# Attention with a three-way maxout layer on one core: another order of the work in batch 0

## The chip, the core and the metric

The kernel runs on one core of a Trainium2 chip. Five engines work side by side, each through its own instructions in order: TensorE (PE in the profile; its weight loads are PEld), VectorE (DVE), ScalarE (ACT), GpSimd (POOL) and SyncE (SP, which here only issues DMAs). They wait for each other by semaphores. The metric is the device time of one execution in microseconds, the median of the runs.

## The reference

q, k and v have 8 batches, 12 heads, 448 rows and a head dimension of 64, in float32. An attention whose denominator has one more term, exp(-m), is followed by a maxout layer of width 768:

```python
scores = scale * np.matmul(q, k.transpose(0, 1, 3, 2))
m = np.max(scores, axis=-1, keepdims=True)
e = np.exp(scores - m)
attn = e / (np.sum(e, axis=-1, keepdims=True) + np.exp(-m) + 1e-09)
attn_out = np.matmul(attn, v)          # (8, 12, 448, 64)
x = attn_out.transpose(0, 2, 1, 3).reshape(8 * 448, 12 * 64)
h = np.maximum(np.maximum(x @ w1, x @ w2), x @ w3)
out = h @ w_out                        # (3584, 768)
```

Multiplied by exp(m), the quotient is exp(scores) over (sum of exp(scores) + 1). The kernel computes it so, without a maximum, and the + 1 is the bias of a logarithm.

## The kernel before, in words

The 96 heads are worked in 48 pairs, six pairs to a batch. One round of the loop (`it`, L452) computes the scores of pair `it` and the attention products of the pair before it (`prev`). From it 6 on, products of the maxout layer of finished batches are put between the attention steps ("groups", L443), and PE is nearly always busy. In batch 0 (its 0 to 5) there is no such work yet. `keep_busy` (L345) puts products of a zero tile into PE there, 13 at the start, 3 after the first transposes, and 3 in each of its 0 to 4; their results are not used.

The 448 rows of a head are seven chunks of 64. Three full blocks of 128 rows, c = 0, 1, 2, and one last block of 64 rows are treated apart. A pair in batch 0 passes through these steps:

- `load` (L83): each of q, k and v comes with two DMAs, one for each half of the partitions. All are issued by SP, in program order, but for two at the very start that ACT issues. Pairs 1 and 2 share their v load, and pairs 4 and 5 share their loads. The raw tiles hold three pairs each and there are three of them, so pairs 0 to 2, 3 to 5 and 6 to 8 have a tile of their own.
- `casts` (L161): DVE turns q (L183), k (L184) and two small last blocks of k (L189) into 16 bits; POOL scales v (`scaled`, L157), with three operations.
- `transposes` (L204): PE transposes q and k block by block into PSUM (L221, L226), and DVE copies the result into qkT (L233). Pair 0's copy is split between DVE (L230) and ACT (L231).
- `scores` (L235) for each c: two products (L239), one a head, then `exp_scores` (L248) on ACT over both heads. `scores_last` (L251, product L255) and `exp_last` (L264) do the last block.
- `sums_main` and `sums_last` (L313, L324): six products and one closing product each, first for the denominators (`den`), then with v (`av`).
- `reciprocals_one` (L333): on ACT, the logarithm of (den + 1) into `lnd`, and exp of its negative into `rb`.
- `normalize_one` (L340): DVE multiplies av by rb into xT, the input of the maxout layer.

PSUM has two buffers for the scores (`ps_s`, used in turn by scores and scores_last), two that den and av share (`ps_av`, used in turn), and two for transposes, keep_busy and the maxout products (`ps_u`). qk16, the input of the transposes, has two buffers; vst, the scaled v, three.

An it of batch 0 before the change has this order in the program, and so on each engine: casts of the next pair; scores and exps of c = 0 and 1; den products of the pair before; score c = 2; av products; scores_last; both closing products; exp of c = 2; exp_last; logarithm and reciprocal; transposes of the next pair; keep_busy; normalize_one of the pair before. In it 5, three up products of the maxout layer follow the transposes, then the attention products of pair 5 itself.

The weights come on POOL's own DMA queue (`load_weight`, L144): the first in halves in its 3 and 4, the others in its 5, 6 and 8. POOL issues them in order with its scaling of v. In its 3 and 4, DVE clears a part of the raw q tile (L462) and SP then loads pairs 7 and 8 (and v of pair 6 in it 3).

Of the kernel before, what the change touches and what calls it, by code (L numbers as in the profile page):

```python
# [12 lines left out]
AF = mybir.ActivationFunctionType  # L13
# [8 lines left out]
def kernel(  # L22
# [11 lines left out]
    nc = tc.nc  # L34

    B, H, S, D = q.shape
# [6 lines left out]
    NPAIR = H // 2  # L43
# [39 lines left out]
    def load(p0, n_pairs, names="qkv", engs=(nc.sync, nc.sync)):  # L83
        b, j = divmod(p0, NPAIR)
        tiles = raw[(p0 // HB) % NRAW]
        h0 = 2 * (p0 % HB)
        for name, t, src in zip("qkv", tiles, (q, k, v)):
            if name not in names:
                continue
            rows = src[b, 2 * j : 2 * (j + n_pairs)].rearrange("h (p c) d -> p h c d", c=TP)  # L90
            hs = slice(h0, h0 + 2 * n_pairs)
            engs[0].dma_start(out=t[0:64, hs, 0 : NB + 1, :], in_=rows[:, :, 0 : NB + 1, :])
            engs[1].dma_start(out=t[64:128, hs, 0:NB, :], in_=rows[:, :, NB + 1 : TP, :])
# [7 lines left out]
    load(2, 1, "qk")  # L101
    load(1, 2, "v")
    load(3, 1, "qk")
    load(4, 2, "q")
    load(3, 1, "v")
    load(4, 2, "k")
    load(4, 2, "v")

    idle = cpool.tile([128, S], MMDT, name="idle")
# [51 lines left out]
    def casts(p):  # L161
        cast_qk(p)
        scale_v(p)
# [40 lines left out]
    def transposes(p):  # L204
        odd = (p // NPAIR) % 2
        qkT = att_pool.tile([2 * D, 1024], MMDT, tag="qkT", bufs=3)
        qkTs[p] = qkT, 0, S
        if p >= P_DMA:
            nc.sync.dma_start_transpose(
                out=qkT.rearrange("q (c p) -> q c p", p=128),  # L210
                in_=qk16[p % NK].rearrange("p c h d -> p (c h d)"),
            )
            qkTs[p] = qkT, 64 * odd, 512
            return
        trT = ps_u.tile([128, 1024], MMDT, tag="u", name="trT")


        order = (NB, 0, 1, 2) if odd else (0, 1, 2, NB)
        n0 = 0
        for c in order:  # L220
            nc.tensor.transpose(  # L221
                out=trT[:, n0 : n0 + 128], in_=q16[p % NK][:, c], identity=ident16
            )
            n0 += SL if c == NB else 128
        for c in range(NB + 1):
            nc.tensor.transpose(  # L226
                out=trT[:, S + c * 128 : S + c * 128 + 128], in_=k16[p % NK][:, c], identity=ident16
            )
        if p == 0:
            nc.vector.tensor_copy(out=qkT[:, 0 : S + 128], in_=trT[:, 0 : S + 128])  # L230
            nc.scalar.copy(out=qkT[:, S + 128 : S + 512], in_=trT[:, S + 128 : S + 512])  # L231
        else:
            nc.vector.tensor_copy(out=qkT[:, 0 : S + 512], in_=trT[:, 0 : S + 512])  # L233

    def scores(p, c):  # L235
        qkT, q0, k0 = qkTs[p]
# [11 lines left out]
    def exp_scores(p, c, stp):  # L248
        nc.scalar.activation(out=eT[:, p % 2, c], in_=stp[:, :, 0:S], func=AF.Exp, scale=scale)  # L249
# [80 lines left out]
            stop=True,  # L330
        )

    def reciprocals_one(den):  # L333
        lnd = small.tile([128, S], FP32, tag="lnd")
        rb = small.tile([128, S], FP32, tag="rb")
        nc.scalar.activation(out=lnd, in_=den[:, 0:S], func=AF.Ln, bias=1.0)
        nc.scalar.activation(out=rb, in_=lnd, func=AF.Exp, scale=-1.0)
        return rb

# [5 lines left out]
    def keep_busy(n):  # L345

        ps = ps_u.tile([128, 512], FP32, tag="u", name="busy")
        for _ in range(n):
            nc.tensor.matmul(out=ps[:, 0:S], lhsT=idle[:, 0:128], rhs=idle, start=True, stop=True)  # L349
# [95 lines left out]
            queue.pop(0)()  # L445

    LEFT = 4
    keep_busy(13)
    casts(0)
    transposes(0)  # L450
    keep_busy(3)
    for it in range(NP + 1):  # L452
        p = it if it < NP else None
        prev = it - 1 if it > 0 else None
        to_next = NPAIR - it % NPAIR
        n_groups = -(-max(len(queue) - LEFT, 0) // to_next) if it % NPAIR else 4
        n_groups = max(3, min(5, n_groups))

        first = {3: 1, 4: 2}.get(it)
        if first is not None:  # L460
            hs = slice(2 * first, 2 * first + 2)
            nc.vector.memset(raw[2][0][64:128, hs, NB - 1 : NB + 1, :], 0.0)  # L462
            if first == 1:
                load(NPAIR, 1, "v")
            load(NPAIR + first, 1)
        if it in (3, 4):
            load_weight(0, it - 3)
        if it in (5, 6, 8):
            load_weight((5, 6, 8).index(it) + 1)
        if it < NPAIR:  # L470

            casts(it + 1)
            for c in range(2):
                exp_scores(p, c, scores(p, c))
            if prev is None:
                keep_busy(3)
                exp_scores(p, 2, scores(p, 2))
                transposes(1)
                exp_last(p, scores_last(p))
            else:  # L480
                den, av = (ps_av.tile([128, 512], FP32, tag="av", name=n) for n in ("den", "av"))
                sums_main(prev, den, 1)
                stp = scores(p, 2)
                sums_main(prev, av, 0)
                stl = scores_last(p)
                sums_last(prev, den, 1)
                sums_last(prev, av, 0)
                exp_scores(p, 2, stp)
                exp_last(p, stl)
                rb = reciprocals_one(den)  # L490
                transposes(it + 1)
            if it < NPAIR - 1:
                keep_busy(3)
            else:

                ups = [up_open()]
                up_part(ups[0], 0, 0, 0, range(3))
                av5 = ps_s.tile([128, 2, 512], FP32, tag="s", name="av5")
                sums_main(p, av5[:, 1], 1)
                sums_main(p, av5[:, 0], 0)  # L500
                sums_last(p, av5[:, 1], 1)
                sums_last(p, av5[:, 0], 0)
                rb5 = reciprocals_one(av5[:, 1])
            if prev is not None:
                normalize_one(prev, av, rb)
            if it == NPAIR - 1:
                normalize_one(p, av5[:, 0], rb5)
                batch_done(0)
        elif it == NPAIR:
            exp_scores(p, 0, scores(p, 0))  # L510

            up_part(ups[0], 0, 0, 0, (3,))
            ups.append(up_open())
            up_part(ups[1], 0, 0, 1, range(4))
            ups.append(up_open(ps_av, "av"))
            up_part(ups[2], 0, 0, 2, range(4))
            for dc in (4, 5):
                for fc, ps in enumerate(ups):
                    up_part(ps, 0, 0, fc, (dc,))
                    if dc == 5:  # L520
                        up_close(ps, 0, 0, fc)
            del queue[0:3]
            exp_scores(p, 1, scores(p, 1))
            group()
            casts(it + 1)
            exp_scores(p, 2, scores(p, 2))
            exp_last(p, scores_last(p))
            group()
            transposes(it + 1)
            group()  # L530
        else:
            late = it + 1 < P_DMA
            if not late:

                if it + 2 < NP:
                    cast_qk(it + 2)
                    transposes(it + 2)
                if it + 1 < NP:
                    scale_v(it + 1)
            if p is not None:  # L540
                for c in range(2):
                    exp_scores(p, c, scores(p, c))
            group()
            if late:
                casts(it + 1)
            avs = [av_main(prev, hh) for hh in range(2)]
            av_last(prev, avs)
            if p is not None:
                stp = scores(p, 2)
                stl = scores_last(p)  # L550
            rb = reciprocals(prev, avs)
            if p is not None:
                exp_scores(p, 2, stp)
                exp_last(p, stl)
            if late:
                transposes(it + 1)
            group()
            normalize(prev, 0, avs, rb)
            group()
            normalize(prev, 1, avs, rb)  # L560
            if it % NPAIR == 0:
                batch_done(prev // NPAIR)
            if it + 2 == P_DMA:
                cast_qk(it + 2)
                transposes(it + 2)
            for _ in range(n_groups - 3):
                group()

        for n in range(NPAIR + HB, 2 * NPAIR) if it == NPAIR else (it + 5,):
            if it >= NPAIR and n < NP:  # L570
                load(n, 1)
# [32 lines left out]
```

## Time and profile before

| | |
|---|---|
| median of 3 runs | 367.61 us (367.52 to 367.77) |
| the profiled execution's own time | 367.07 us |
| its span, from first to last instruction | 365.3 us |
| granted TensorE clock, mean | 0.999 |
| PE busy in the span | 357.4 us |
| ACT busy in the span | 221.1 us |
| first exp of pairs 0 to 5 starts at | 7.64, 10.79, 15.09, 19.39, 23.69, 27.99 us |
| transposes of pair 6 start at | 30.52 us |
| first score of pair 6 starts at | 33.37 us |

Times inside the profile are counted from the start of the span. The profile's page gives busy times of engines and groups of instructions; the timeline lists instructions of one engine in order (start, length, engine, line, operation, shapes, count, and in brackets the idle time before and what ended it); the chain of waits follows back from the last instruction what released each step. A group of several pipelined instructions has one length, from the first one's start to the last one's end. Landing is when a DMA's data has arrived.

The loads of batch 0 as the DMA view has them (issue to landing): k of pair 2 landed at 10.91 us, k of pair 3 at 15.18, q of pairs 4 and 5 at 17.64, v of pair 3 at 18.52, k of pairs 4 and 5 at 21.18, their v at 22.81, k of pair 6 at 27.50. The halves of the first weight were issued by POOL at 19.67 and 23.98 and landed at 27.49 and 33.09; the second weight was issued at 25.96, landed at 40.82, and its first product ran at 42.50.

### The profile page before, as it was taken

Reading aid. Unit: us, or ns where it says so; the run is one execution under the profiler, and the core shown is the slowest. Engines: PE = TensorE matmul, PEld = TensorE weight load, DVE = VectorE, ACT = ScalarE, POOL = GpSimd, SP = SyncE. Lnnn points to the kernel's source line nnn. Section 1 sums busy time; section 2 is a strip of 40 time slices with the busy share of each in tenths; the row PEclk is TensorE's granted clock in tenths of the full one; section 3 lists DMA queues with packets and bytes.
Section 4 is the critical chain, followed back from the end, with each engine's and each line's share of the span. In section 5 each row is a group of like instructions: output and inputs, shape, how many; then the busy total and the mean of one; then the engine's idle time right before and its main releaser. Section 6 shows DMA issues by size and latency. Waiting matters only on the chain.

```text
span 365.3 us, 6122 instructions
## 1 busy us (share of the span) xinstructions
PE 357.4 (98%) x2086; PEld 163.9 (45%) x2086; DVE 243.4 (67%) x521; ACT 221.1 (61%) x335; POOL 53.6 (15%) x159
## 2 busy tenths in 40 slices
PE   8999999999999999999999999999999999999995
PEld 3434444444444444444444444444444444445552
DVE  4474777876578677577657867757666776555553
ACT  4996476765666766666567666666566766651000
POOL 4263112211211211211121121121112112000000
PEclk9999999999999999999999999999999999999999
DMA  5999997668667888849764896758675673005006
GB/s 151 229 234 229 233 247 211 155 177 214 161 180 182 208 184 154 195 107 185 182 173 122 178 200 164 175 133 214 159 174 137 165 208 83 5 2 131 2 0 172
DMA packets 87951, 58.61 MB, mean 160 GB/s; under 512 B 43504, under 2 KB 84464, under 8 KB 87920
## 3 DMA queue, kind: packets, MB, share of 16 engines
q1 hardware_dynamic: 83632, 53.18, 59.7%
q0 software_dynamic: 3920, 4.72, 7.5%
q10 hardware_dynamic: 368, 0.33, 0.4%
q8 instruction: 16, 0.26, 0.3%
q14 instruction: 15, 0.12, 0.1%
HBM read 42.47 MB, written 11.01 MB: 146 GB/s over the span
## 4 chain that ended last, share of the span: by engine, by line
PE 91%; ACT 2%; DMA 2%; DVE 2%; issue 1%; SPq 0%; DVEq 0%
PE up L356 44%; PE op L390 15%; PE av L273 13%; PE stp L239 8%; PE stl L255 4%; PE av L285 3%; DMA kin<-in_k_dram 2%; PE busy L349 2%; ACT eT L249 1%; PE trT L221 1%; PE trT L226 1%; PE av L316 1%; DVE qkT L233 1%; DVE o_sb L415 0%; DVE qk L183 0%
## 5 line engine op out<-in xcount | busy, mean ns | idle before, releaser
L356 PE MATMUL up<-xT,w 128*128 128x448 f16 x864 | 175.3, 353 | 0.7 <-DVE xT L307 0.4
L249 ACT ACTIVATE eT<-stp 128x896 f16<-128x896 f32 x144 | 125.5, 910 | 53.3 <-PE stp L239 53.3
L356 PEld LDWEIGHTS <-w 128*128 128x128 f16 x864 | 81.7, 98 | 81.7 <-issue 12.5
L372 DVE TENSOR_TENSOR hT<-hT,up 128x448 f16<-128x448 f16 x96 | 59.6, 621 | 52.1 <-PE up L356 51.1
L157 POOL TENSOR_SCALAR vst<-vin 128x384 f16<-128x384 f32 x132 | 43.1, 338 | 255.2 <-issue 159.2
L298 ACT ACTIVATE lnd<-av 64x448 f32<-64x448 f32 x84 | 45.3, 539 | 49.0 <-PE av L285 48.0
L390 PE MATMUL op<-w,hT 128*128 128x384 f16 x336 | 59.3, 326 | 0.0
L273 PE MATMUL av<-eT,vst 128*128 128x448 f16 x252 | 54.5, 352 | 0.0
L307 DVE TENSOR_TENSOR xT<-av,rb 64x448 f16<-64x448 f32 x84 | 51.8, 617 | 1.4
L239 PE MATMUL stp<-qkT 64*128 64x448 f16 x288 | 44.1, 353 | 1.5 <-DVE qkT L233 0.7
L370 DVE CAST hT<-up 128x448 f16<-128x448 f32 x48 | 29.8, 624 | 22.9 <-PE up L356 22.2
L415 DVE TENSOR_SCALAR o_sb<-op 128x384 f32<-128x384 f32 (+1 forms) x56 | 30.8, 550 | 20.0 <-PE op L390 19.0
L390 PEld LDWEIGHTS <-hT 128*128 128x128 f16 x336 | 31.6, 98 | 24.7 <-issue 4.0
L273 PEld LDWEIGHTS <-vst 128*128 128x128 f16 x252 | 24.7, 98 | 22.4
L184 DVE CAST qk<-kin 128x384 f16<-128x384 f32 x47 | 25.7, 548 | 1.1 <-DMA kin<-in_k_dram 0.7
L265 ACT ACTIVATE eL<-stl 128x448 f16<-128x448 f32 x48 | 25.9, 539 | 0.0
L299 ACT ACTIVATE rb<-lnd 128x448 f32<-128x448 f32 x42 | 24.2, 576 | 1.3
L239 PEld LDWEIGHTS <-qkT 64*128 64x128 f16 x288 | 11.0, 94 | 23.2 <-issue 16.5
L419 ACT ACTIVATE o_sb<-op 128x192 f32<-128x192 f32 x1 | 0.3, 331 | 30.2 <-DVE o_sb L415 30.2
L189 DVE CAST qk<-kin 64x64 f16<-64x64 f32 x94 | 17.5, 187 | 1.3
L255 PE MATMUL stl<-qkT 128*128 128x448 f16 x48 | 17.4, 362 | 0.0
L285 PE MATMUL av<-eL,vst 64*128 64x448 f16 x84 | 15.2, 359 | 0.0
(50 smaller groups left out, 117.7 us busy)
## 6 DMA issues: line engine op xcount, KB each, us to landing
out_dram<-o_sb SPq DMA_DIRECT2D x54, 192.0 KB, 2.8
qin<-in_q_dram SPq DMA_DIRECT2D x46, 128.0 KB, 3.0
kin<-in_k_dram SPq DMA_DIRECT2D x45, 128.0 KB, 2.9
vin<-in_v_dram SPq DMA_DIRECT2D x44, 128.0 KB, 2.9
kin<-in_k_dram SPq DMA_DIRECT2D x46, 96.0 KB, 2.7
qin<-in_q_dram SPq DMA_DIRECT2D x45, 96.0 KB, 2.7
vin<-in_v_dram SPq DMA_DIRECT2D x44, 96.0 KB, 2.8
w<-in_moe_w_dram POOLq DMA_DIRECT2D x2, 1152.0 KB, 17.1
```

The lines of the kernel that those rows point to most:

```text
L157: nc.gpsimd.tensor_scalar(out=out, in0=in_, scalar1=LAMBDA, scalar2=1.0, op0=ALU.mult, op1=ALU.mult)
L239: nc.tensor.matmul(out=stp[:, hh, 0:S], lhsT=qkT[hh * D : hh * D + D, k0 + c * 128 : k0 + c * 128 + 128], rhs=qkT[hh * D : hh * D + D, q0 ...
L249: nc.scalar.activation(out=eT[:, p % 2, c], in_=stp[:, :, 0:S], func=AF.Exp, scale=scale)
L255: nc.tensor.matmul(out=stl[:, 0, 0:S], lhsT=qkT[:, k0 + NB * 128 : k0 + NB * 128 + 128], rhs=qkT[:, q0 : q0 + S], start=True, stop=True,)
L273: nc.tensor.matmul(out=av[:, 0:S], lhsT=vst[:, p % VB, hh * NB + c, (1 - hh) * D : (3 - hh) * D], rhs=eT[:, p % 2, c, hh, :], start=(c == ...
L298: nc.scalar.activation(out=lnd[mine], in_=avs[hh][other, 0:S], func=AF.Ln, bias=1.0)
L307: nc.vector.tensor_tensor(out=xTs[b][mine, j, :], in0=avs[hh][mine, 0:S], in1=rb[mine], op=ALU.mult)
L356: nc.tensor.matmul(out=ps[:, 0:S], lhsT=w_sb[i][:, dc, ts(fc, 128)], rhs=xTs[b][:, dc, :], start=(dc == 0), stop=(dc == NDC - 1),)
L370: nc.vector.tensor_copy(out=h, in_=ps[:, 0:S])
L372: nc.vector.tensor_tensor(out=h, in0=h, in1=ps[:, 0:S], op=ALU.max)
L390: nc.tensor.matmul(out=ps[:, 0:NW], lhsT=hTs[sb][:, fc, ts(t, 128)], rhs=wout_sb[:, fc, ts(nh, NW)], start=(fc == 0), stop=(fc == NFC - 1),)
L415: nc.vector.tensor_scalar(out=o_sb[:, cs], in0=src, scalar1=1.0 / LAMBDA, scalar2=None, op0=ALU.mult)
```

## The change

It does five things, all in batch 0.

1. Load order: k of pairs 4 and 5 is asked for together with their q, ahead of v of pair 3. Pair 8 is loaded, and its part of the raw q tile cleared, in it 5 and no longer in it 4.
2. In its 1, 2 and 4, the next pair's transposes stand between the third score and the av products. In its 3 and 5 ("late") they stand behind the logarithm.
3. The first score and first exp of the next pair are done at the end of the it, the exp between the logarithm and the reciprocal. Each it then begins with c = 1.
4. normalize_one of the pair before is put off to the next it, in the late ones ahead of the casts, else behind them. In it 5, both outstanding normalizations come at the end, and the three up products come behind the attention products of pair 5.
5. The keep_busy products of its 1 to 4 are gone; it 0 has three groups of two in place of one of three, and its transposes come ahead of the third score. The copy of pair 4's transposes is cut into two.

```diff
-    load(4, 2, "q")
+    load(4, 2, "qk")
     load(3, 1, "v")
-    load(4, 2, "k")
     load(4, 2, "v")
...
-            nc.vector.tensor_copy(out=qkT[:, 0 : S + 512], in_=trT[:, 0 : S + 512])
+            cut = S + 128 if p == NPAIR - 2 else S + 512
+            for cols in (slice(0, cut), slice(cut, S + 512)):
+                if cols.start < cols.stop:
+                    nc.vector.tensor_copy(out=qkT[:, cols], in_=trT[:, cols])
...
-        first = {3: 1, 4: 2}.get(it)
+        first = {3: 1, 5: 2}.get(it)
...
+            if it == 0:
+                casts(1)
+                exp_scores(0, 0, scores(0, 0))
+                exp_scores(0, 1, scores(0, 1))
+                keep_busy(2)
                 transposes(1)
+                exp_scores(0, 2, scores(0, 2))
+                keep_busy(2)
+                exp_last(0, scores_last(0))
+                keep_busy(2)
+                exp_scores(1, 0, scores(1, 0))
             else:
+                late = it in (3, NPAIR - 1)
+                if waiting is not None and late:
+                    normalize_one(*waiting)
+                casts(it + 1)
+                if waiting is not None and not late:
+                    normalize_one(*waiting)
+                exp_scores(p, 1, scores(p, 1))
                 den, av = (ps_av.tile([128, 512], FP32, tag="av", name=n) for n in ("den", "av"))
                 sums_main(prev, den, 1)
                 stp = scores(p, 2)
+                if not late:
+                    transposes(it + 1)
                 sums_main(prev, av, 0)
                 stl = scores_last(p)
                 sums_last(prev, den, 1)
                 sums_last(prev, av, 0)
                 exp_scores(p, 2, stp)
                 exp_last(p, stl)
-                rb = reciprocals_one(den)
-                transposes(it + 1)
-            if it < NPAIR - 1:
-                keep_busy(3)
-            else:
-                ups = [up_open()]
-                up_part(ups[0], 0, 0, 0, range(3))
+                lnd = log_one(den)
+                if late:
+                    transposes(it + 1)
+                if it < NPAIR - 1:
+                    exp_scores(it + 1, 0, scores(it + 1, 0))
+                    waiting = prev, av, exp_one(lnd)
+            if it == NPAIR - 1:
+                rb = exp_one(lnd)
                 av5 = ps_s.tile([128, 2, 512], FP32, tag="s", name="av5")
                 sums_main(p, av5[:, 1], 1)
                 sums_main(p, av5[:, 0], 0)
                 sums_last(p, av5[:, 1], 1)
                 sums_last(p, av5[:, 0], 0)
-                rb5 = reciprocals_one(av5[:, 1])
-            if prev is not None:
+                ups = [up_open()]
+                up_part(ups[0], 0, 0, 0, range(3))
+                rb5 = exp_one(log_one(av5[:, 1]))
                 normalize_one(prev, av, rb)
-            if it == NPAIR - 1:
                 normalize_one(p, av5[:, 0], rb5)
```

`log_one` and `exp_one` are the two halves of `reciprocals_one`.

More of the change, by code (lines that the diff above doesn't have):

```diff
@@ L331, in sums_last, with log_one, exp_one @@
         )
-    def reciprocals_one(den):
+    def log_one(den):
         lnd = small.tile([128, S], FP32, tag="lnd")
+        nc.scalar.activation(out=lnd, in_=den[:, 0:S], func=AF.Ln, bias=1.0)
+        return lnd
+    def exp_one(lnd):
         rb = small.tile([128, S], FP32, tag="rb")
-        nc.scalar.activation(out=lnd, in_=den[:, 0:S], func=AF.Ln, bias=1.0)
         nc.scalar.activation(out=rb, in_=lnd, func=AF.Exp, scale=-1.0)
@@ L447 @@
     LEFT = 4
+    waiting = None
     keep_busy(13)
@@ L470 @@
         if it < NPAIR:
[L472 to L475, printed above, removed]
-                keep_busy(3)
-                exp_scores(p, 2, scores(p, 2))
-                transposes(1)
-                exp_last(p, scores_last(p))
-            else:
+            if it == 0:
[3 more added lines that the diff above has]
+                keep_busy(2)
+                transposes(1)
+                exp_scores(0, 2, scores(0, 2))
[3 more added lines that the diff above has]
+                exp_scores(1, 0, scores(1, 0))
+            else:
+                late = it in (3, NPAIR - 1)
[5 more added lines that the diff above has]
+                exp_scores(p, 1, scores(p, 1))
                 den, av = (ps_av.tile([128, 512], FP32, tag="av", name=n) for n in ("den", "av"))
@@ L489 @@
                 exp_last(p, stl)
-                rb = reciprocals_one(den)
-                transposes(it + 1)
-            if it < NPAIR - 1:
-                keep_busy(3)
-            else:
-                ups = [up_open()]
-                up_part(ups[0], 0, 0, 0, range(3))
+                lnd = log_one(den)
[6 more added lines that the diff above has]
+                rb = exp_one(lnd)
                 av5 = ps_s.tile([128, 2, 512], FP32, tag="s", name="av5")
```

## The prediction

> **What bounds the kernel now.** I read the page first, then TensorE's granted clock in stretches, then the chain of waits inside batch 0, then the timelines of single engines. The page says that this is a TensorE kernel:
>
> ```profile
> span 365.3 us, 6122 instructions
> ...
> PE 357.4 (98%) x2086; PEld 163.9 (45%) x2086; DVE 243.4 (67%) x521; ACT 221.1 (61%) x335; POOL 53.6 (15%) x159
> ```
>
> From 31 us on PE hardly stops. So batch 0 (its 0 to 5) can only shift all that follows, and its worth is read at one place: when does PE begin transposes(6), from which on PE is full? In the timeline that is 30.52 us now. The chain of waits over one period, start and length of each piece:
>
> ```profile
> 18.01 0.24 PE trT L226 x4
> 18.24 0.02 issue
> 18.27 0.67 DVE qkT L233
> 18.94 0.05 issue
> 18.98 0.38 PE stp L239 x2
> 19.36 0.02 issue
> 19.39 0.93 ACT eT L249
> 20.31 0.04 issue
> 20.36 0.37 PE stp L239 x2
> 20.72 0.69 PE av L316 x6
> 21.41 0.30 PE stl L255
> 21.70 0.19 PE den L325
> 21.89 0.19 PE av L325
> 22.08 0.22 PE trT L221 x4
> 22.31 0.24 PE trT L226 x4
> ```
>
> It repeats after 4.30 us and is neither PE's nor ACT's sum: it is one round of transposes, copy, first score, first exp, third score, products, transposes. ACT is close behind: its timeline of the same period has 0.28 us idle.
>
> ```profile
> 19.39 2.53 ACT L249 ACTIVATE eT<-stp 128x896 f16<-128x896 f32 x3 [0.28 <-PE stp L239]
> 21.80 0.56 ACT L265 ACTIVATE eL<-stl 128x448 f16<-128x448 f32 x1
> 22.22 0.57 ACT L336 ACTIVATE lnd<-den 128x448 f32<-128x448 f32 x1
> 22.83 0.58 ACT L337 ACTIVATE rb<-lnd 128x448 f32<-128x448 f32 x1
> ```
>
> **Prices, all from these rows.** Exp: next one after 0.805 ((2.53-0.92)/2), result after 0.92. Last exp to logarithm 0.42. Logarithm to another exp: estimated 0.45 (0.57 less the same overlap). Reciprocal: 0.58, next after 0.48 (34.05 to 34.53). normalize_one 0.62. A pair of scores: next after 0.29, result 0.38. Six products 0.69. scores_last: result 0.36. Each closing product 0.19. Transposes 0.45, copy may begin after 0.65; copy 0.66. Casts of a pair on DVE 1.2 (0.35, 0.46, 0.39 to the next). A wait between engines 0.03 to 0.05.
>
> **What goes.** The transposes leave the old round in its 1, 2 and 4. The 15 keep_busy products of its 0 to 4 (0.73 a group of three) become 6 in it 0. They fill time in which PE waits for the copy (busy ends near 18.65, scores at 18.98), so on the path they are worth nothing.
>
> **What is late next.** normalize_one(prev) now runs one it later, its reciprocal behind the next pair's first exp; and av has two buffers shared with den, so the av products of an it wait for that normalization. PE is in order: behind these products stand scores_last, both closing products and the next first score. New round, from logarithm to logarithm: 0.45 + exp 0.805 + reciprocal 0.58 + 0.03 + normalize 0.62 + 0.05 + products 0.69 + scores_last 0.36 + 0.03 + last exp 0.42 = **4.03** us. ACT alone needs 3 x 0.805 + 0.42 + 0.45 + 0.48 = 3.77, so it does not bind. The round saves 0.27 a period where nothing else is late. Start of the first exp of each pair (1 to 5: 10.79, 15.09, 19.39, 23.69, 27.99 before):
>
> - Pair 1: copy(1) is early; scores(1,0) wait for the buffer of exp(0,2), done 10.20. First exp 10.65 (-0.14).
> - Pair 2: nothing to normalize. k of pair 2 lands at 10.91, casts end 11.9, transposes to 12.4, av to 13.1, last exp 13.47, logarithm 13.9, exp **14.35** (-0.74).
> - Pair 3: casts(3) stand ahead of normalize on DVE and k of pair 3 lands at 15.18 (the landing is SP's issue order, unchanged so far): casts end 16.14, normalize 16.72, av to 17.46, last exp 17.85, logarithm 18.27, exp **18.72** (-0.67).
> - Pair 4 (it 3, "late"): normalize ends 20.75, av to 21.5, closing products to 22.07; only then transposes(4), half copy (0.46, as L230) at 22.72, scores 23.24, exp **23.65** (-0.05). casts(4) run 20.65 to 21.9 and are just covered.
> - Pair 5 (it 4): 23.65 + 4.03 = **27.68** (-0.31).
> - it 5 ("late"): reciprocal from 28.49, normalize 29.1 to 29.72, av 29.77 to 30.46, scores_last and closing products to **31.03**, then transposes(6), against 30.52: before, av began at 29.25 because nothing had to be normalized first.
>
> So transposes(6) come **+0.51** later. casts(6) follow normalize on DVE and end at 30.85, covered by 0.2.
>
> Now the cover. The query cast took 0.42 alone, and 0.73, 0.60 and 0.77 in its 3 to 5, each time beside POOL work (scale_v or a weight issue). In the new order casts(4) meet scale_v(3) and the weight issue, and casts(6) may meet the issue at 29.4. With +0.31 each, cover is lost by 0.16 in it 3 and about as much in it 5: **+0.83**. [...]
>
> After transposes(6) PE's work to scores(6,0) is the same (three up products only change place), with no new wait: PE takes 1.26 + 0.38 + 0.57 us there and the last normalizations are ready 1.9 us after the av5 products, before dc 4 is reached 2.6 us after them. The pieces take 0.0 to 0.1 more where a product restarts after a wait and may take as much less: +-0.2 over the five periods. I take the middle of 0.51 and 0.83, with a little less for the second collision: +0.6.
>
> **The loads.** k of pairs 4 and 5 now lands ahead of v of pair 3: about 19.6 to 20.3 instead of 21.18; nobody waits longer. v of pair 3 lands at 20.5 to 21.2 instead of 18.52; its first use (av in it 4, 25.7) is far. But on POOL's queue the first half of w0 stands behind scale_v(3): issued at 21.7 to 22.4, not 19.67. In the DMA view its packets ran from 22.0 to 26, 2.3 after the issue; so now from 24.0 to 24.7 until 28.0 to 28.7. The second half's packets began only near 27.3, with the weights' queue nearly empty from 26 on; that hole closes, so the queue behind it slips by 0.7 to 1.4 only. w1 landed at 40.82 (issue 25.96, 14.9 to landing) and is first multiplied at 42.50. New: 41.5 to 42.2, used at 43.1. Covered, and at no cost. Pair 8's load costs nothing: SP reaches it at 28.15 whatever its place in the program, since SP's own queue is that long; its memset on DVE is done by 26.6.
>
> **Sum.** Profiled execution: 367.07 us, span 365.3 and 1.8 around it. 367.07 + 0.6 = 367.7; the median of the runs is 367.61, 0.54 above that execution, so **368.2**. 0.2% of it (0.74 us; about what a measurement of this kernel can tell from no change) puts the limits at 366.87 and 368.35.
>
> **Rivals.**
> - *Faster: the normalization is not what av waits for.* If it is ready when PE gets to av, the period is ACT's 3.77 and transposes(6) could come 2.2 us earlier. For: ACT had 0.28 idle, and PE's own work is 3.2 a period. Against: the reciprocal cannot be earlier than a whole exp after the logarithm. It decides where normalize ends before the third score does. The gain is capped: w1 cannot land before about 41.5, so 42.50 moves by 1.0 at most: 366.6 to 367.3. Chance 0.19.
> - *The clock gate.* Stretches of the span (length, busy PE, granted clock, DMA):
>
> ```profile
> 22.94:26.36 3.42, 3.10 (x25) 1.00 1.23 227
> 26.36:29.77 3.41, 3.09 (x30) 1.00 1.17 245
> 360.86:364.27 3.41, 0.00 (x0) 1.00 0.78 214
> 364.28:365.28 1.00, 0.00 (x0) 0.50 0.00 0
> ```
>
>   Before, no such stretch of batch 0 had under 3.09 of 3.41 us busy; the clock halved only after a stretch with none. Without the keep_busy products, its 2 to 4 have 2.2 to 2.8 of 3.41. Where between 0 and 3.09 the limit lies no row shows. At half clock a period's 3.2 of PE work takes 6.4 against 4.03: over one 3.4 us stretch some 1.7 us lost, after which PE is full again. One or two such: 369.9 to 371.6. Chance 0.12. [...]
> - *w1 late.* If the whole slip of w0 (2.0 to 2.7) reached w1, it would land at 42.8 to 43.5 and hold PE up to 0.4: 368.3 to 368.6. Against it stands the hole that closes. Chance 0.07.
> - *The change does not do what it says* holds for pair 8 alone, as worked out: no time.
>
> **How the numbers follow.** As worked out: 0.62, own range 367.9 to 368.6, 0.40 of it within 0.2% and 0.22 above. Faster rival 0.19: 0.14 beyond 0.2%, 0.05 within. Clock 0.12 and w1 0.07: slower. Together faster 0.14, same 0.45, slower 0.41. Leaving out the clock rival and no more, the range is 366.6 to 369.3, the upper end with both cast collisions, a late w1 and the restarts.
>
> **What would show it.** Right: first exps near 10.65, 14.35, 18.7, 23.7 and 27.7; in its 2 to 5 the av products released by normalize_one on DVE, and ACT's last exp held by scores_last after them; transposes(6) near 31.1; w1's products near 43.1 without a wait. Wrong: a granted clock of 0.5 before 31 us; av products that start right behind the third score or the transposes; idle PE before w1's first product; transposes(6) before 30.3.

## The result, and the profile after

| | before | after |
|---|---|---|
| median (8 runs each) | 367.58 us (367.52 to 367.84) | 368.74 us (368.41 to 369.20) |
| ratio, 95% interval | | 1.003 (1.0019 to 1.0041) |
| the profiled execution, its span | 367.07, 365.3 us | 368.52, 366.7 us |
| first exp of pairs 1 to 5 | 10.79, 15.09, 19.39, 23.69, 27.99 | 10.62, 14.44, 19.24, 24.18, 28.22 |
| transposes of pair 6 | 30.52 | 31.59 |
| first score of pair 6 | 33.37 | 34.44 |
| w1: landed, first product | 40.82, 42.50 | 43.90, 43.95 |

The changed kernel is slower by 1.16 us at the median. The forecast was 368.2. Its wide range, 366.6 to 369.3, holds the result; 367.9 to 368.6, the range of the worked-out chain alone, does not. The first two lines of the page, to set beside those of before:

```profile
span 366.7 us, 6101 instructions
...
PE 356.6 (97%) x2074; PEld 164.2 (45%) x2074; DVE 243.3 (66%) x522; ACT 221.0 (60%) x335; POOL 53.9 (15%) x159
```

PE is busy for 0.8 us less, with nine filling products gone, and the span is 1.4 longer. The chain of waits over one round of the changed kernel, from the logarithm at the end of it 2 to scores_last of it 3 (start, length, piece):

```profile
18.92 0.43 ACT lnd L337
19.35 0.81 ACT eT L251
20.16 0.47 ACT rb L342
20.64 0.02 issue
20.66 0.64 DVE xT L348
21.30 0.04 issue
21.34 0.76 PE av L318 x6
22.09 0.30 PE stl L257
```

This is the round that the prediction worked out: logarithm, next pair's first exp, reciprocal, normalization, av products, scores_last. The transposes' copy is no longer in it, DVE's xT (normalize_one) is. In PE's timeline the same wait stands in the bracket: PE began its third score at 20.21, ended it near 20.57 and then sat idle until the normalization was done.

```profile
20.21 0.36 PE L241 MATMUL stp<-qkT 64*128 64x448 f16 x2
21.34 0.76 PE L318 MATMUL av<-eT,vst 128*64 128x448 f16 x6 [0.76 <-DVE xT L348]
```

There are four such waits, 2.15 us together, one in each of its 2 to 5. The next shift falls in it 6, where the changed kernel loses another 0.35: GpSimd's scaling of v of pair 8 met VectorE's small casts of pair 7, because that v had landed at 40.76 and not at 43.17 as before. VectorE's small casts of pair 7 in the kernel before, then one line each from VectorE's, GpSimd's and PE's timelines of the changed kernel:

```profile
39.68 0.39 DVE L189 CAST qk<-kin 64x64 f16<-64x64 f32 x2
```

```profile
40.75 0.74 DVE L188 CAST qk<-kin 64x64 f16<-64x64 f32 x2
...
40.93 1.03 POOL L156 TENSOR_SCALAR vst<-vin 128x384 f16<-128x384 f32 x3 [6.71 <-DMA vin<-in_v_dram]
...
42.20 1.29 PE L361 MATMUL up<-xT,w 128*128 128x448 f16 x6 [0.42 <-DVE hT L375]
```

The two small casts took 0.39 in the kernel before; here 0.74, and the maxout product behind them starts 1.42 us later than before, not 1.07. With that, nearly all of the 1.45 us between the two profiled executions is found.

### The profile page after: what moved, and what is told of

The parts are those of the page before. It is cut to its first block, busy times and chain, and to the rows that moved or that the text cites. A ratio compares the mean times of both kernels' runs of the same rounds, so it can differ in the third digit from the quotient of the medians.

```text
span 366.7 us, 6101 instructions
## 1 busy us (share of the span) xinstructions
PE 356.6 (97%) x2074; PEld 164.2 (45%) x2074; DVE 243.3 (66%) x522; ACT 221.0 (60%) x335; POOL 53.9 (15%) x159
## 4 chain that ended last, share of the span: by engine, by line
PE 87%; DMA 5%; SPq 3%; DVE 2%; ACT 1%; issue 1%; DVEq 0%
PE up L361 44%; PE op L395 15%; PE av L275 13%; PE stp L241 7%; PE av L287 3%; PE stl L257 3%; DMA kin<-in_k_dram 3%; DMA vin<-in_v_dram 2%; SPq L92 2%; SPq L93 1%; ACT eT L251 0%; PE av L318 0%; DVE o_sb L420 0%; DVE xT L348 0%; DVE xT L309 0%
## 5 line engine op out<-in xcount | busy, mean ns | idle before, releaser
L275 PEld LDWEIGHTS <-vst 128*128 128x128 f16 x252 | 24.7, 98 | 22.4
L188 DVE CAST qk<-kin 64x64 f16<-64x64 f32 x94 | 18.3, 194 | 1.3
```

The lines of the kernel that those rows point to most:

```text
L275: nc.tensor.matmul(out=av[:, 0:S], lhsT=vst[:, p % VB, hh * NB + c, (1 - hh) * D : (3 - hh) * D], rhs=eT[:, p % 2, c, hh, :], start=(c == ...
```

## The experiments

Twelve kernels, in three groups; each was timed beside the kernel before, whose median was 367.70, 367.59 and 367.56 us in the three groups. Two theories stood at first. **A**: the time is lost in the new order, since av waits for a normalization that was put off. **B**: it is lost because v of pair 3 is loaded later, GpSimd's queue with it, and so the second weight. They became one, **C**: two bounds, one behind the other.

**loads_only** and **order_only** take the change apart. The first is the kernel before with

```diff
-    load(4, 2, "q")
+    load(4, 2, "qk")
     load(3, 1, "v")
-    load(4, 2, "k")
...
-        first = {3: 1, 4: 2}.get(it)
+        first = {3: 1, 5: 2}.get(it)
```

and the second the changed kernel with these lines as before.

> The kernel before with the new load order alone (k of pairs 4 and 5 ahead of v of pair 3; pair 8's clearing and load in it 5). Theory A (the time lost lies in the order of the work: av waits for a normalization put off): nothing is lost, 367.4 to 367.8 us, transposes(6) at 30.5. Theory B (the weights are late: w1 lands at 43.9 in the changed kernel, while the kernel before multiplies it at 42.5): transposes(6) still at 30.5, but PE waits some 1.4 before w1's first product, 368.7 to 369.1. I hold both to be true, the later of the two setting the time, so 368.9.

Measured: 368.13 us, ratio 1.002 (1.0003 to 1.0036), single runs from 367.73 to 371.05. Transposes(6) came at 30.78, near the 30.52 of before. PE then waited for w1, as B says; its timeline:

```profile
42.28 0.55 PE L238 MATMUL stp<-qkT 64*128 64x448 f16 x4
44.55 0.74 PE L355 MATMUL up<-xT,w 128*128 128x448 f16 x3 [1.72 <-DMA w<-in_moe_w_dram]
```

The profiled execution took 369.17, so at the median the wait is presumably smaller. The loads alone cost 0.4 us at the median, less than the 1.3 expected, and the single runs lie further apart.

> The changed kernel with the load order of before. Theory A alone: transposes(6) stay near 31.5 and the time 368.3 to 368.8. Theory B alone: w1 lands at 40.8 again and the loss goes, 367.3 to 367.7. Both together: chain +1.0, the collision of casts(7) with GpSimd's work in it 6 (0.35) may go with the earlier v of pair 8: 368.3 to 368.6.

Measured: 368.94 us, ratio 1.0036 (1.0024 to 1.0048). B alone is out: with the old loads the loss stays, though PE did not wait for w1 (landed at 43.83). The loss is a little larger than I expected of A. In its profile k of pairs 4 and 5 landed at 22.24 and it 3 waited 0.45 for the cast, so that transposes(6) came at 32.32; another 0.58 was lost before pair 12's first score, a wait that comes up again below. In the eight profiles with the new order and the new loads this k landed between 19.65 and 21.18, and it 3 did not wait for its cast. The new load order does help the new order of work there.

**own_den** takes away what makes av wait. den goes to the PSUM pool of the transposes, so that av has two buffers:

```diff
-                den, av = (ps_av.tile([128, 512], FP32, tag="av", name=n) for n in ("den", "av"))
+                den = ps_u.tile([128, 512], FP32, tag="u", name="den")
+                av = ps_av.tile([128, 512], FP32, tag="av", name="av")
```

**own_den_old_loads** is the same with the load lines of before.

> The changed kernel with den in a PSUM buffer of the pool that transposes use, so that av has two buffers of its own and its products no longer wait for the normalization of the it before. Theory A alone: transposes(6) near 30.6 (0.95 earlier than in the changed kernel) and 367.6 to 367.9. Theory B alone: 368.7, unchanged. Both: transposes(6) near 30.6, but PE then idles before w1's first product near 43.9: 368.5 to 368.8.

Measured: 369.78 us, ratio 1.0057 (1.0037 to 1.0077): the slowest of all, though batch 0 became faster. Rounds fell to 3.78 and 3.77 (first exps 14.93, 18.71, then 23.10, 26.87), which is ACT's own sum in the prediction, and transposes(6) began at 29.68. Then PE came to w1 2.35 us too early, and behind the idle time the granted clock was at half:

```profile
44.50 2.35 PE L361 MATMUL up<-xT,w 128*128 128x448 f16 x6 [2.35 <-DMA w<-in_moe_w_dram]
46.64 1.98 PE L275 MATMUL av<-eT,vst 128*128 128x448 f16 x6
```

Stretches of own_den: length, busy PE, granted clock, share and GB/s of the DMA engines.

```profile
20.71:24.13 3.42, 2.60 (x25) 1.00 0.90 215
...
41.19:44.60 3.42, 1.07 (x8) 1.00 1.15 233
44.60:48.02 3.42, 3.42 (x10) 0.50 1.15 232
```

While the clock was at half, six av products took 1.98 us and not 1.30. So this run shows both halves of C: the wait for the normalization was the bound of batch 0, and w1 is the next one, with a price of its own.

> The changed kernel with den in its own buffer and the load order of before. Theory A alone: as own_den by it, 367.6 to 367.9. Theory B alone: 367.3 to 367.7, as order_only by it. Both: neither wait is left; transposes(6) near 30.6, w1 in time, 367.5 to 367.8.

Measured: 368.14 us, ratio 1.0012 (1.0003 to 1.0021), above what C said (367.8 at most). Transposes(6) came at 30.42, PE waited 0.22 for w1, and there was a wait that I had not expected: 0.78 before pair 12's first score, for the first DMA transposes. They stand in SP's queue behind a row of loads. In the seven profiles of these experiments that have this wait, SP issued them 0.11 us after it was done with the load ahead of them; in the other seven profiles it issued them 0.06 to 0.07 after VectorE's last cast for them.

The second group tried to free the transfers: pair 8 cleared and loaded in it 6, the third weight issued in it 7.

```diff
-        first = {3: 1, 5: 2}.get(it)
+        first = {3: 1, 6: 2}.get(it)
...
-        if it in (5, 6, 8):
-            load_weight((5, 6, 8).index(it) + 1)
+        if it in (5, 7, 8):
+            load_weight((5, 7, 8).index(it) + 1)
```

> own_den with less traffic beside the weights: pair 8 is cleared and loaded in it 6 (so SP's queue, pairs 9 to 11 included, stands still from about 27 to 35) and the third weight is issued in it 7, not 6. Theory C (two bounds: the chain through the normalization, and behind it the landing of w1): w0 and w1 have the transfers nearly to themselves, w1 lands near 38, no wait before its first product, transposes(6) at 29.1 to 29.7: 366.3 to 366.8, faster than both kernels. Rival D (without the keep_busy products and with PE idle in pieces, the granted clock falls or something else takes the gain): 367.6 or more.

Measured: 367.95 us, ratio 1.0015 (0.9997 to 1.0033). A miss. w1 landed at 41.59, not near 38, and was in time; transposes(6) at 29.59. The gain was then lost before pair 12's first score.

> The changed kernel with the same later load of pair 8 and later third weight; av still waits for the normalization. Theory C: w1 has time to spare, the chain alone is left: transposes(6) near 31.5, 368.3 to 368.7, hardly better than the changed kernel. If the weights were the whole cause: 367.3 to 367.6.

Measured: 368.90 us, ratio 1.0041 (1.0023 to 1.0059); transposes(6) at 31.51, w1 used at 43.49 without a wait, and 0.34 of wait at pair 12. Transposes(6) are as late as in the changed kernel, so the chain's part is there without w1, as C says. The time alone does not show it, for the control that follows loses almost as much by the move of the loads.

> The kernel before with the same later load of pair 8 and later third weight, a control. Theory C: w1 was not waited for there, so no change, 367.4 to 367.8. Any other result would mean that the move itself is worth something.

Measured: 368.67 us, ratio 1.0036 (1.0019 to 1.0053). A miss: the move has a price of 1.08 us at the median, and after_late_p8 is only 0.23 slower than this control. SP issues the last load of pair 8 at 38.49 and not at 31.65, its loads near 60 us still come some 2 us later, and the DMA transposes wait their turn. PE in the control, then in own_den_late_p8:

```profile
74.29 0.55 PE L239 MATMUL stp<-qkT 64*128 64x448 f16 x4 [0.95 <-DMA qkT<-qk]
```

```profile
73.80 0.55 PE L241 MATMUL stp<-qkT 64*128 64x448 f16 x4 [1.52 <-DMA qkT<-qk]
```

In their profiles neither the kernel before nor the changed one has this wait. It is a third bound, behind the other two.

**own_den_late_p8_early_t6** changes one line more, `late = it == 3`.

> own_den_late_p8 with it 5 in the order of the others (casts ahead of the normalization, transposes of pair 6 between the third score and the av products). With den in its own buffer nothing needs the normalization early, and casts(6) no longer stand behind it on VectorE. Theory C: 0 to 0.4 better than own_den_late_p8, 366.0 to 366.8. If casts(6) wait for k of pair 6 the gain is nothing or up to 0.3 is lost, since PE then waits ahead of av and not behind it.

Measured: 367.93 us, ratio 1.001 (0.9993 to 1.0027): a miss, and the same as without it. Transposes(6), now ahead of av, came at 28.06, with 1.02 us of wait at pair 12 and 0.64 at w1 behind them. What batch 0 had won was taken by these two transfers.

The third group brings w1 in halves, which moves no load of q, k and v:

```diff
-            load_weight((5, 6, 8).index(it) + 1)
+            for half in (0, 1) if it == 5 else (None,):
+                load_weight((5, 6, 8).index(it) + 1, half)
```

> The changed kernel with the second weight brought in two halves, as the first one is, so that its first product needs only the half that lands some 4 us earlier (near 40). Theory C: w1 no longer holds PE in any run, the chain through the normalization is left: transposes(6) near 31.5, 368.3 to 368.6, and a smaller spread than the changed kernel's 0.8. If the landing of w1 were the main loss: 367.5 to 367.8.

Measured: 368.23 us (368.02 to 368.57), ratio 1.0017 (1.0008 to 1.0026). The first half landed at 41.26, its use came at 43.67. This is the order of the work with w1 out of the way: +0.67 us, near the +0.6 of the prediction, and 0.5 less than the changed kernel's median. In its profile the small casts of it 6 took 0.39 again. The intervals of the two overlap, so the 0.5 is the likely share of w1 and of the collision in it 6, not a shown one; the profiled execution of the changed kernel itself met w1 with 0.05 to spare.

> own_den with the second weight in two halves. Theory C, with the third bound that the last runs showed (SP's queue: the first DMA transposes, of pair 12, stand behind a backlog of loads and land near 74): transposes(6) at 29.1 to 29.7, no wait for w1, no halved clock, but a wait of 0.5 to 1.5 before pair 12's first score: 367.0 to 367.6. Without that third bound: 366.2 to 366.6.

Measured: 366.93 us (366.33 to 367.52), ratio 0.998 (0.9971 to 0.9988): faster than both kernels. It differs from after_w1_halves in den's buffer alone and is 1.30 us faster, with intervals that do not overlap: this is the price of the wait for the normalization when w1 is out of the way. ACT's timeline of one round, where the logarithm follows the last exp and nothing is idle until pair 4's copy:

```profile
17.85 0.54 ACT L267 ACTIVATE eL<-stl 128x448 f16<-128x448 f32 x1
18.29 0.54 ACT L337 ACTIVATE lnd<-den 128x448 f32<-128x448 f32 x1
18.71 0.92 ACT L251 ACTIVATE eT<-stp 128x896 f16<-128x896 f32 x1
19.51 0.59 ACT L342 ACTIVATE rb<-lnd 128x448 f32<-128x448 f32 x1
19.98 1.74 ACT L251 ACTIVATE eT<-stp 128x896 f16<-128x896 f32 x2
```

What is left of waits for transfers is 0.20 at the second half of w0 and 0.28 at pair 12.

**own_den_w1_halves_loads_later** and **before_w1_halves_loads_later** add

```diff
-        for n in range(NPAIR + HB, 2 * NPAIR) if it == NPAIR else (it + 5,):
+        for n in range(NPAIR + HB, 2 * NPAIR - 1) if it == NPAIR else (it + 4,):
```

> own_den_w1_halves with the loads of pairs 11 and on asked for one it later, so that pair 14's six loads stand behind pair 12's transposes in SP's queue and not ahead of them. Theory C: no wait is left at w1 nor before pair 12's first score, the 1.2 us won in batch 0 reach the end: 366.2 to 366.8, faster than both kernels. If the loads are then late elsewhere: 367 or more.

Measured: 367.38 us, ratio 0.9997 (0.9988 to 1.0006). A miss: the wait at pair 12 went, and another came, further on:

```profile
85.45 3.56 PE L361 MATMUL up<-xT,w 128*128 128x448 f16 x18 [0.72 <-DVE hT L375]
```

> The kernel before with the second weight in two halves and the loads of pairs 11 and on one it later, a control. Theory C: it waited for neither, so no change: 367.4 to 367.8. If it gains as much as the kernel above, that gain is not from the order in batch 0.

Measured: 368.80 us, ratio 1.0037 (1.0024 to 1.0049). The control pays the same kind of wait (0.82, PE for VectorE's o_sb), and 0.7 in it 3 for k of pair 4. VectorE's timeline of the control shows the cause of the first: the casts of a pair wait for its k, and the o_sb copies stand behind them.

```profile
77.93 0.56 DVE L184 CAST qk<-kin 128x384 f16<-128x384 f32 x1 [1.52 <-DMA kin<-in_k_dram]
78.40 0.40 DVE L189 CAST qk<-kin 64x64 f16<-64x64 f32 x2
78.82 1.02 DVE L415 TENSOR_SCALAR o_sb<-op 128x384 f32<-128x384 f32 x2
```

## Why the prediction was right, and where it was not

**The bound of batch 0 and its successor: right.** The transposes' copy left the chain, the normalization took its place. The round was given as 4.03 us; measured from logarithm to logarithm 4.05 (18.82 to 22.87), and 4.04 from pair 4 to pair 5. From pair 5's first exp to transposes(6) I had 3.35; it was 3.37. The late it 3 was 4.93 against 4.94. own_den and own_den_w1_halves showed the cause by taking it away.

**Pair 3: 0.4 too early.** k of pair 3 landed at 15.59 and not at 15.18, and the cast began at 15.71. The kernel before had the cast start at 15.73 behind the normalization and so never showed this landing as a wait. In the new order casts, transposes, normalization and av all hang on it: pair 2 to pair 3 took 4.80, 4.74 and 4.77 in the three profiles of changed order and loads, against 4.37 worked out. I took a landing for a fixed time: in the fourteen profiles this one lay between 15.12 and 15.75, with a like spread under both load orders.

**Casts beside GpSimd: wrong in place.** I charged 0.16 in each of its 3 and 5 to the query casts. In the changed kernel's profile they took 0.42 in both. In it 3 v of pair 3 came later than I had it, and its scaling (GpSimd, 0.51 us from 22.17 on) met the small casts instead:

```profile
22.00 0.73 DVE L188 CAST qk<-kin 64x64 f16<-64x64 f32 x2
```

These took 0.73 and not the 0.40 of its 0 to 2 and 5, so it was not the query cast alone that grew beside GpSimd's work; nothing waited for them. In after_w1_halves the query cast of it 5 did take 0.78, and pair 5's first exp was still followed by transposes(6) after 3.36. The cover was larger than I had counted: I took it up to the first transposes (22.61 in it 3), but those of k, which need the last casts, come 0.22 later. The +0.6 that I forecast was therefore the chain's +0.51 plus a term that cost nothing, while the landing above gave 0.5 instead; that the range still held the result is partly luck. A collision did cost 0.35, in it 6, where I had not looked.

**The loads: wrong, and the weakest step.** "Covered, and at no cost" was said of w1. The term that failed is the slip of the weights' queue: v of pair 3 landed at 22.00, not 20.5 to 21.2, and the first half of w0 was issued at 23.14, not 21.7 to 22.4. The step that k of pairs 4 and 5 lands earlier held for its first half only (18.95); the second half landed at 21.18 as before. w1 came at 43.90, not 41.5 to 42.2. Of the 3.47 us by which that half was issued later, 3.08 reached w1; the hole in the weights' queue, which was to take up 1.3 us, took up 0.4. In the changed kernel's profile it cost nothing only because PE, too, came later than forecast (43.95, not 43.1). I gave this rival 0.07; loads_only and own_den show that it decides as soon as batch 0 is not slower. Its price was also too small there, for I had not joined it with the clock.

**Pair 8: right on its load, not on its cost.** Its first DMA was issued at 27.20, against 28.15 before. But its v landed 2.4 us earlier, and so came the collision in it 6. No run separates the move of pair 8 from the new order of the other loads.

**The clock: right to give it a small chance.** The prediction left open what lies between 0 and 3.09 us of busy PE. The changed kernel's emptiest stretch of batch 0:

```profile
19.37:22.78 3.41, 2.56 (x21) 1.00 1.01 241
```

The clock was at full there, with PE busy for 2.56 of 3.41 us, and at full from 5.71 us to the end of the span; six waits of PE of 0.2 to 0.8 us within 15 us did not lower it. In own_den a stretch with 1.07 us busy was followed by 3.42 us at 0.50.

**The size.** +0.6 forecast, +1.16 measured, +0.67 with w1 out of the way. The profiled execution of before, against which I summed, is 0.5 under its own median, so that the difference of the two profiled executions (1.45) overstates the change. Where the 0.5 arises is not shown, but it 3 is a likely place. In the profile of before, k of pairs 4 and 5 landed at 21.18 and no transpose waited for its cast. In before_late_p8 and before_w1_halves_loads_later, with the same order of the work and of these loads, it landed at 21.45 and 22.00, and from pair 3's first exp to pair 4's it took 4.76 and 5.29, not 4.30. That round of it 3 was thus one draw, at a place where a landing is the next bound.

## What to carry to other kernels

When a step is moved off the chain that sets the end, follow the buffers of the step that it is moved behind: here a normalization put off by one round kept an accumulator, and the accumulator kept TensorE. Before counting a gain, ask of the next two or three transfers how much they have to spare and by how much their landings vary; here own_den was 1.91 us ahead of the changed kernel at transposes(6) (29.68 against 31.59), and then waited 2.35 us for w1. Splitting that transfer, so that its first user needs only half, was worth more here (own_den 369.78, with w1 in halves 366.93) than moving loads about, which twice paid for one wait with another.

## What the runs showed of the hardware

- One load, at the same place in the queue, landed at different times from one profile to the next. The second half of pair 3's v, in the old load order, was issued at 14.86 or 14.87 in the profiles of the kernel before, own_den_old_loads and order_only (the kernels differ, the loads ahead of it do not) and landed at 18.52, 19.21 and 20.33; the weight issue behind it on GpSimd moved with it (19.67, 20.35, 21.64), and w1 landed at 40.82, 42.66 and 43.83.
- The profile's record of the full clock begins at 5.88 us in the kernel before, at 5.71 in the changed kernel and at 7.06 in own_den; pair 1's first exp was at 10.79, 10.62 and 11.11. In the kernel before, 13 products of the zero tile from 1.16 us on took 4.94 us, and three of the same shape from 6.51 on took 0.73. So 0.5 us of a comparison of these single executions can be the start.
- In own_den, behind the wait of 2.35 us, the clock was at 0.50 from 44.60 to 48.02 us, though PE was busy for all of that stretch.
- What came ahead of a lower clock, and what did not, in stretches of 3.41 to 3.42 us: the clock was at 0.50 right behind a stretch with PE busy for 1.07 us (own_den, 41.19 to 44.60) and behind one with none (the kernel before, 360.86 to 364.27). It was at full behind one with 1.57 us (the changed kernel, 360.70 to 364.11, followed by 2.6 us to the end of the span). loads_only, with its wait of 1.72 us, had a mean granted clock of 1.000 over its profiled execution, own_den 0.995.
